# Cosformer attention and a gated layer on one core: q, k, v of batch 0 also cast to fp16 by GpSimd's loads, first products by 128 tokens, normalising in three steps

## The chip, the cores and the metric

The kernel runs on one core of one Trainium2 chip. A core has TensorE (PE, matmuls; its weight loads are listed as PEld), VectorE (DVE), ScalarE (ACT), GpSimd (POOL) and SyncE (SP); SP, ACT and POOL can issue DMAs, and all DMAs share 16 DMA engines. The metric is the device time of one execution in microseconds (us), the median of several runs. Lower is better.

## The reference

q, k, v are fp32 of shape 8 batches x 8 heads x 576 tokens x 64. The result is 4608 x 512 in fp32.

```python
def phi(x, c, s):                                  # c, s: cos and sin of pi/2 * token / 576
    r = np.maximum(x, 0.0)
    return np.concatenate([r * c, r * s], axis=-1) # 64 -> 128 features
q_p, k_p = phi(q, cos_w, sin_w), phi(k, cos_w, sin_w)
kv  = np.einsum('bhsf,bhsd->bhfd', k_p, v)
z   = np.sum(k_p, axis=2)
num = np.einsum('bhsf,bhfd->bhsd', q_p, kv)
den = np.einsum('bhsf,bhf->bhs', q_p, z)[..., None] + 1e-06
x   = (num / den), heads side by side              # 4608 tokens x 512
h   = x @ w_in                                     # 512 -> 2048
out = (h * np.cos(h)) @ w_out                      # 2048 -> 512
```

## The kernel before

**Tiling.** A batch's 576 tokens are 4 tiles of 128 tokens and a rest of 64; the rests of two batches share a fifth tile (t = 4). Layer 1 and layer 2 are done batch by batch in chunks c = 0 to 7 of 512 tokens, and a ninth chunk holds all the rests. Inside SBUF a token block of five or four tokens lies on each partition, so a load of q, k or v is two DMAs: `five` (5 tokens on 64 partitions) and `four` (4 tokens on the other 64). What the missing fifth token leaves is set to zero.

**Attention of a batch.** `load` (L264) brings q, k, v. `prep` (L286) computes relu times cos or sin, one instruction for a token tile and one of the two feature halves, on ACT or DVE, and writes fp16 into KQ. `cast_v` (L300) copies v into V1, which has a column of ones for z. `kv` (L311) multiplies k with V1, 40 matmuls (L319), and copies the result to kvz. q must be transposed: in batches 0 and 1 by PE (`q_pe`, L348, and a copy of the result by ACT or DVE, L352 or L354), from batch 2 on by a transposing DMA that SP issues (`q_dma`, L358). `num` (L365) computes numerators and denominators (L380) into PSUM and normalises: `norm` adds 1e-6 to the denominators (L412), takes reciprocals (L414) and multiplies (L405), one step of the plan, all on DVE. `x_pe` (L430) or `x_dma` transposes x into xT.

**Layers.** In chunks 0 and 1 `layer1` (L473) takes two 128-column blocks of w_in and half of the tokens (256) at a time: 8 matmuls of 256 columns (L493) into a bank of PSUM. `gate` (L464) computes the cosine on ACT (L467) and multiplies on DVE (L469). From chunk 3 on, parts of layer 1 and all of layer 2 are done with 7 products in place of 8 (L620, L796). Stores of the result are issued by POOL (L683).

**Batch 0.** Its q, k, v (in that order, `ORDER0`) are loaded as fp32 by SP into tiles that are used for something else later (`raw0`, L206 to L209). All other loads of q, k, v are issued by POOL and cast to fp16 on the way, as are w_in (`weights`, L873, four DMAs of a quarter) and w_out (`w_out_load`, L884). A small copy on POOL (`hold`, L875), which waits for batch 0's k, stands ahead of w_in's loads. POOL sets S2, V1 and MINUS at the beginning (L855, L860, L861).

**Dummy matmuls.** `warm` (L866) runs matmuls on constants: 14 at the beginning, 16 behind the q transposes of batch 0, and 4, 3 and 2 between the numerators of batch 0 (`FILL`).

**What sets the order.** Each step is recorded in a plan with its cost, due time and what it reads and writes. The list `ORDER` of 1348 words, written into the file, fixes the order of all steps, and for steps that may run on two engines, the engine. Each engine works its instructions in order. POOL's DMAs use 8 semaphores in turn, so a DMA can wait for the landing of the one eight before it.

Of the kernel before, what the change touches and what calls it, by code (L numbers as in the profile page):

```python
# [10 lines left out]
AF = mybir.ActivationFunctionType  # L11
ALU = mybir.AluOpType
# [5 lines left out]
POW = False  # L18
FAST = ((3, 2), (4, 2), (5, 2), (6, 4), (7, 4), (8, 4))
ORDER = (  # L20
    "1 6 1 -3 4 -6 7 1 1 1 1 1 18 1 -5 -7 -1 14 -5 -4 107D 1A -109 6 -25 17 -19 33 1D 8A 92 -136 "
    "38A 4D 93 -92D -3A 5D -31 27A -2D -24 22D 10A 3A -1D -3D 2A -23 -9 37D 2A -1D 2 -4A -1D 86 "
    "-115 35 1 -32 -9 42 -29 30 -26 27 77 -75 -1 -44 49 -1 3 -1 72 -76 9 -8 7 3 -1 67 -71 8 -7 8 "
    "1 59 -63 7 -6 65 9D -18 -49 63D 1D -67 62 -57 -4 3 71D -12 -55 -2 62D -61 4 -2 1 4 -2 57D "
    "-56 4 -2 58D -57 4 -2 54D -53 4 -2 50D -49 4 -2 50D -49 4 -2 175 -122D -4A -48 4 171 -173 "
    "63D -58 -2 -2 3 2 2 43A 4D -48 4 -2 38D -33 -4 2 55D -54 4 -2 53A -2D -50 36 -34 54 -14A 13D "
    "-52 4 47D -1D -21 6D 123 -104 -24 4 6D -3 18 -12D -2 -3 117 -93 -20 15 4 -5 101 -112 13 23 "
    "75 -110 17 -47 51 -1 -7 24 -68 45 8 14 710 -721 13 -8 90D -89 716 -721 -3 -5 100D -79 -20 8 "
    "86A 2A 2D 4D -93 88A -84 26 64A -81 73D -85 267 -272 95D 4D 117 -207 91D -69 -21 207 -182 "
    "82D -15 -70 188 -183 -19 15 75A 113 -120 -65 2 2 681 -617A -65 4 -2 73D -72 4 -2 66D -5A -60 "  # L30
    "4 -2 59 -27 24 -51 -36 91D -86 32 -5 61 -59 30 144A -205 32 60A 118A -175 58 1A -32 -26 61A "
    "-1 -54 -41 202A -4 -196 34 2 60 112A -11 -162 62 1 -61 -32 94 106A 6A -151 43 -1 -2 103A "
    "-200 101 -64 61 -63 172A -102 -104 38 159D -160 4 -2 311 -145A -165 63 -2 -59 2 158D -97 95A "
    "-153 55 244 -303 2 63 1 -3 4 -62 -51 119 101A -100 -4 232 -238 4 238 -299 62 -66 3 159 -157 "
    "161D 3A -67 -96 159A -209 140 78A -7 -99 31 -2 6 65D -95 27 -2 72 2A -68 59 12D -101 90 148D "
    "-136 135D -134A -76 4 -36 104 -62 -5 72A 135D -132 -73 -1 5 67 123 12D -134 -71 4 1 187 5A "
    "-196 10 -48 110 -230 163 2 190A -349 158 67 2 -64 -44 -2 230A -121 -61 63 -68 197A -235 42 "
    "65 -68 69 1 -65 5 61 119A -183 4 -5 66 117A -116 1 -115 53 -4 67 122A -184 69 109A -172 57 "
    "-67 5 314 -250 -118 117 -62 -53 239A 130 -252 -59 2 305 -123A -121 -67 7 309 -311 178 -182 7 "
    "-186 364A -238 54 187A -91 6 -4 2 88 -249 241 -79 91A -73 66 -82 -158 161 -40 38 4 -46 128D "  # L40
    "-83 -160 150 12 -4 5 -11 21 -8 -45 55 200A -133A -68 -172 375A -131D -245 2 244 2A -85 208A "
    "-188 -18 -159 237 -9 -231 163 2 -48 -115 2 240A -78 81 -83 84 113 -239 59 -176 -4 122 126 "
    "-77 203A -256 241 -187 -55 134 -245 363A -119 -65 188A -197 -10 -47 133 112A 149 -332 -61 53 "
    "9 71 -248 119 1 49 71 -59 68 -131 132 111A -240 49 8 66 -60 174D -107 -69 -59 60 196A -13D "
    "-114 2 -75 74 -60 -71 133 -83 -48 70 -9 71 -70 -61 1 61 193A -7D -185 -61 254 -21D -165 168A "
    "-173 -17 -44 60 315 -313 11 175A 126 -311 190A -186 -68 255A -184 87 -89 91 88A -86 -92 173 "
    "-168 171D -174 175 -83 -88 87 -157 67 185A -8 -85 -163 255A -98 7 76 -113 127 -75 63 -114 38 "
    "91 -252 162 216A -382 169 -5 -159 253 -91 90 -251 173 -50 130 -91 -161 123 256A -206 201A "
    "-223 -156 259 -90 -1 20 186 -204 90 -71 -59 131 -90 -172 180 202A -255 246 -110 2 -70 189A "
    "-210 200 -201 23 68 -5 -73 -11 -45 69 67 -134 49 197A -202 91 2 -1 -133 47 5 199D 1A -251 "  # L50
    "134 -79 -58 250A -112 -88 9 196A -250 50 -4 -50 63 76 -75 74 -133 238A 2D -179 -63 64 335 "
    "-351 8 12 69 -134 1 396 -142A -253 60 338 -334 186D -184 -5 -9 347 -334 4 -2 -5 200A -15 13A "
    "-188 91 -93 -2 183A -176 184D -188 181 -85 -91 89 83 -247 167 -95 96 92 -97 99D -90 235A "
    "-238 -163 247A -180 100 1 80 1D -254 75 99 -5 -37 45 -46 116 -241 398A -226 85 138A -226 -5 "
    "-169 254A -79 -169 257 -262 254 -72 -175 256 -130 50 -6 -176 183 -48 26 230 -261 6 256 -128 "
    "-131 -2 -130 177 -44 131 -88 2 5 213A -204 -13 5 -46 127 -72 -54 260A -214 83 -128 127 -69 "
    "197D -126 -75 5 -13 219A -210 75 1 1 -85 -51 66 -2 -4 213D -147 -121 132 -72 214A -226 214D "
    "-137 150A -228 16 190A -191 -59 130 -84 15 213A -207 -20 15 52 146D -196 -11 -52 256A 16 "
    "-210 2 -67 277D -199 -77 67 2 -66 68 196A -12D -177 -4 -4 198 -196 -78 269 7A 7 -268 270A "
    "-206 2 94 -90 190A -98 -6 -161 72 94 101 -105 98 -92 18 75 -130 42 -41 52 -10 -168 179 -22 "  # L60
    "-30 44 10 91 -421 420 -113 7 108 -87 -20 18 -183 168 3 96A -266 273 1 -106 -41 56 92 -114 12 "
    "12 -192 181 -12 114 -105 15 -192 283 1 -103 -47 144 -276 191 10 -68 -134 284 -84 73 -80 8 -4 "
    "-66 75 79 -87 -63 68 83 -109 -38 69 -14 13 -71 63 10 78 -102 -47 83 -84 82 -24 -9 -46 148 "
    "-68 -10 -69 1 69 -7 85 -67 69 -75 -20 16 5 10 -82 68 15 -23 20 -7 -75 83 -3 6 94 -179 180 "
    "-93 -1 -16 76 39 -105 103 -95 3 93 -182 69 21 -88 -1 86 -84 88 88 23 -18 16 -20 7 14 -113 "
    "101 17 -199 196 -15 -42 44 -182 199 -203 181 23 -61 46 16 -61 43 -182 201 -18 -38 -5 45 -334 "
    "337 14 1 -14 -193 146 44 4 17 -3 6 -2 -31 35 -1 -2 -63 67 16 49 -62 -29 -44 74 13 -10 -79 3 "
    "74 -23 40 -16 12 -35 -48 88 -87 83 -235 217 7 1 -17 -203 235 -14 16 -1 39 -127 90 -14 53 "
    "-132 136 -56 14 -90 77 -76 128 -74 75 -128 129 2 -39 -91 133 -45 4 43 -1 -41 -92 69 -9 87 "
    "-12 -65 75 -9 10 -145 77 59 -49 60 3 -13 14 -150 151 -64 53 -134 135 -64 -70 84 -90 7 120 14 "  # L70
    "-140 90 60 -15 -127 143 9 -8 -310 250 69 -34 -126 156 5 -4 -155 150 -8 14 7 -159 86 74 -13 9 "
    "16 -9 -2 -77 90 -12 -74 85 -44 35 1 10 -86 -2 43 39 -78 87 -183 95 90 -32 -56 47 40 -30 -56 "
    "89 -88 72 -71 75 11 -10 -75 61 26 -16 17 -26 -60 70 -71 91 -12 -77 86 4 -88 89 -4 -86 2 75 "
    "-71 -3 4 84 -87 88 5 -89 -3 82 11 -88 90 -1 -5 -85 86 6 -8 15 -12 7 6 -7 3 5 -6 2 8 -7 8 -4 "
    "5 1 1 -6 10 -9 8 -2 1 3 1 1 1 1 1 1 "
)


class Plan:


    def __init__(self):
        self.steps = []
# [940 lines left out]
```

## Time and profile before

| | |
|---|---|
| median of 3 runs | 280.96 us (278.95, 280.96, 282.47) |
| the profiled execution's own time | 283.07 us |
| its span, first to last instruction | 281.3 us |
| PE, PEld busy | 269.9 us (96%), 216.4 us (77%) |
| DVE, ACT, POOL busy | 251.8 us (90%), 210.5 us (75%), 60.3 us (21%) |
| mean granted TensorE clock | 0.994 |
| DMA queue of POOL (q0) | 29856 packets, 28.12 MB |
| DMA queue of SP (q1) | 47840 packets, 14.95 MB |

How to read it: times inside the profile count from the span's start. The span and the time of the same execution differ by 1.77 us, which lie around the span. PE's busy time is modelled from pipelined matmuls and is not PE at its peak. MB of a casting load are those written, half of those read. The granted clock is the share of TensorE's full speed that it was allowed.

### The profile page before, as it was taken

To read this page: it belongs to the slowest core of one execution; us is meant where nothing else is said; L and a number is where in the kernel's file an instruction comes from. 1 tells how busy PE (TensorE), PEld (TensorE's weight loads), DVE (VectorE), ACT (ScalarE), POOL (GpSimd) and SP (SyncE) were. 2 spreads that over 40 slices of the span, in tenths; PEclk is the share of its full clock that TensorE was granted. 3 is DMA by queue.
4 is the path that set the end of the run, shared out by engine and by line. 5 is a ranking of instruction groups with operands and counts; after the bars stand their busy time and mean duration, and the time that the engine had idled before them with its cause. 6 is when DMAs were issued, how large, how long until landed. Compare 5 with 4: busy or idle time off the path is not lost.

```text
span 281.3 us, 6759 instructions
## 1 busy us (share of the span) xinstructions
PE 269.9 (96%) x2691; PEld 216.4 (77%) x2691; DVE 251.8 (90%) x484; ACT 210.5 (75%) x353; POOL 60.3 (21%) x98
## 2 busy tenths in 40 slices
PE   7799999998999799999999999999999999999994
PEld 2568876865956478787878787779988888888883
DVE  2879999897999799999999999999999999988952
ACT  2856876898899969889899987987576776657420
POOL 1472141410403300502323030002110220121300
PEclk9799999999999999999999999999999999999999
DMA  6999999999999999999999999486850434075124
GB/s 208 327 201 203 201 190 177 184 147 185 125 188 156 193 226 145 193 172 156 210 199 107 179 189 161 77 166 150 192 94 2 87 107 125 3 224 114 75 77 149
DMA packets 78463, 44.06 MB, mean 157 GB/s; under 512 B 46176, under 2 KB 75360, under 8 KB 78432
## 3 DMA queue, kind: packets, MB, share of 16 engines
q0 software_dynamic: 29856, 28.12, 57.5%
q1 hardware_dynamic: 47840, 14.95, 30.9%
q10 hardware_dynamic: 736, 0.57, 0.6%
q8 instruction: 21, 0.34, 0.5%
q14 instruction: 10, 0.08, 0.1%
HBM read 36.74 MB, written 9.44 MB: 164 GB/s over the span
## 4 chain that ended last, share of the span: by engine, by line
PE 82%; DMA 9%; DVE 5%; ACT 2%; issue 1%; SPq 0%; ACTq 0%
PE M L796 33%; PE M L620 14%; PE M L525 8%; DMA qT<-KQ 7%; PE TR L620 6%; PE M L493 4%; PE M L722 4%; PE ATT L380 3%; DVE gT L469 3%; PE ATT L319 3%; DMA gT<-in_q_dram 2%; PE TR L525 2%; PE M L348 2%; PE ATT L870 1%; ACT KQ L295 1%
## 5 line engine op out<-in xcount | busy, mean ns | idle before, releaser
L796 PEld LDWEIGHTS <-gT 128*128 128x128 f16 x560 | 54.1, 98 | 7.6
L295 ACT ACTIVATE KQ<-RAW,CS 128x512 f16<-128x512 f16 x86 | 59.1, 720 | 0.0
L796 PE MATMUL M<-w_out_sb,gT 128*128 128x256 f16 x448 | 56.2, 273 | 0.0
L467 ACT ACTIVATE ch<-M 128x512 f32<-128x512 f32 x75 | 44.1, 598 | 13.2 <-PE M L493 4.4
L469 DVE TENSOR_TENSOR gT<-M,ch 128x512 f16<-128x512 f32 x73 | 49.1, 684 | 3.1 <-ACT ch L467 2.3
L525 PE MATMUL M<-xT,w_in_sb 128*128 128x512 f16 x136 | 33.1, 379 | 0.0
L796 PE MATMUL M<-TT,S 128*128 128x256 f16 x256 | 32.0, 273 | 0.0
L807 ACT ACTIVATE ost<-M 128x512 f32<-128x512 f32 x32 | 19.1, 597 | 17.2 <-PE M L796 13.4
L493 PE MATMUL M<-xT,w_in_sb 128*128 128x256 f16 x256 | 29.7, 272 | 0.0
L683 POOL DMA_DIRECT2D out_dram<-ost x32 | 18.8, 611 | 47.2 <-DVE ost L811 25.7
L620 PEld LDWEIGHTS <-w_in_sb 128*128 128x128 f16 x264 | 25.4, 98 | 3.7
L796 PEld LDWEIGHTS <-S 128*128 128x128 f16 x256 | 24.6, 98 | 3.0
L628 ACT ACTIVATE Z<-M 128x512 f32<-128x512 f32 x31 | 18.2, 600 | 11.6 <-PE M L620 8.6
L493 PEld LDWEIGHTS <-w_in_sb 128*128 128x128 f16 x256 | 24.6, 98 | 3.0
L632 DVE TENSOR_TENSOR Z<-M,Z 128x512 f32<-128x512 f32 x38 | 25.4, 683 | 1.1 <-PE M L620 0.6
L525 PEld LDWEIGHTS <-w_in_sb 128*128 128x128 f16 x160 | 14.8, 98 | 13.1
L405 DVE TENSOR_TENSOR x<-ATT,rec 128x512 f16<-128x512 f32 x32 | 22.1, 691 | 1.1
L380 PEld LDWEIGHTS <-qT 128*128 128x128 f16 x320 | 15.7, 98 | 7.3 <-DMA qT<-KQ 3.7
L811 DVE TENSOR_TENSOR ost<-M,ost 128x512 f32<-128x512 f32 x24 | 16.4, 684 | 4.2 <-PE M L796 4.0
L380 PE MATMUL ATT<-kvz,qT 128*128 128x65 f16 x288 | 16.4, 194 | 3.0 <-DMA qT<-KQ 2.6
L296 DVE TENSOR_SCALAR KQ<-RAW,CS 128x512 f16<-128x512 f16 x54 | 18.3, 350 | 0.2 <-DMA RAW<-in_k_dram 0.2
L773 DVE TENSOR_TENSOR S<-gT 128x2048 f16<-128x2048 f16 x14 | 17.0, 1217 | 0.1
(133 smaller groups left out, 482.3 us busy)
## 6 DMA issues: line engine op xcount, KB each, us to landing
out_dram<-ost POOLq DMA_DIRECT2D x32, 256.0 KB, 4.7
RAW<-in_k_dram POOLq DMA_DIRECT2D x7, 320.0 KB, 5.3
RAW<-in_q_dram POOLq DMA_DIRECT2D x7, 320.0 KB, 7.6
w_in_sb<-in_moe_w_in_dram POOLq DMA_DIRECT2D x4, 512.0 KB, 9.8
w_out_sb<-in_moe_w_out_dram POOLq DMA_DIRECT2D x4, 512.0 KB, 12.1
RAW<-in_v_dram POOLq DMA_DIRECT2D x6, 320.0 KB, 7.4
RAW<-in_k_dram POOLq DMA_DIRECT2D x7, 256.0 KB, 6.4
RAW<-in_q_dram POOLq DMA_DIRECT2D x7, 256.0 KB, 6.7
```

What stands on the lines that cost most here:

```text
L295: fn = {"ACT": lambda: nc.scalar.activation(out=out_, in_=in_, func=AF.Relu, scale=sc), "DVE": lambda: nc.vector.tensor_scalar(out=out_, i ...
L380: nc.tensor.matmul(bank[hb][:, hh * D1:(hh + 1) * D1], lhsT=a[:, h, :], rhs=z[:, h, :], start=(i == 0), stop=(i == len(parts) - 1))
L405: nc.vector.tensor_tensor(out=split(x16[n][:, hs, :], k), in0=A[:, :, :, 0:D], in1=split(rec[n][:, hs], k).unsqueeze(3).broadcast_to((P, k ...
L467: act(0.5, due, lambda: nc.scalar.activation(out=ch[c], in_=bank, func=AF.Sin, bias=math.pi / 2.0, scale=1.0), [key], [("ch", c)])
L469: mul(due, 0.61, lambda q: q.tensor_tensor(out=dst, in0=bank.rearrange("p (j s) -> p j s", j=2), in1=ch[c].rearrange("p (j s) -> p j s", j ...
L493: nc.tensor.matmul(M1[m][:, jj * 2 * P:(jj + 1) * 2 * P], lhsT=w_in_sb[:, cc, j * P:(j + 1) * P], rhs=X[:, cc, ts], start=(cc == 0), stop= ...
L525: nc.tensor.matmul(M, lhsT=w_in_sb[:, cc, j * P:(j + 1) * P], rhs=X[:, cc, :], start=(cc == 0), stop=(cc == NCT - 1))
L620: nc.tensor.matmul(bank[0][:, j * TH:(j + 1) * TH], lhsT=a(cc, j), rhs=b[:, cc, :], start=(first and j == 0 and cc == 0), stop=(last and j ...
L632: dve(0.61, due + 0.3, lambda: nc.vector.tensor_tensor(out=dst, in0=bank[0], in1=dst, op=ALU.add), [bank[1], key], [key])
L683: pl.add(eng, 0.9 if eng == "POOL" else 0.65, 0, due, lambda: q.dma_start(out=dst, in_=src_), keys, [], dma=(nb, 355.0))
L796: nc.tensor.matmul(bank[0][:, tt * MH:(tt + 1) * MH], lhsT=a[:, j, tt * P:(tt + 1) * P], rhs=b[:, j, :], start=(first and (apart or tt == ...
L807: act(0.5, due, lambda: nc.scalar.activation(out=dst, in_=view(bank), func=AF.Copy), [bank[1]], dk)
```

## The change

All loads of q, k, v are now issued by POOL and cast to fp16; `raw0` and the fp32 forms of `prep` and `cast_v` are gone. In batches 0 and 1, v is loaded by halves of the heads (as batch 1's was before) and q in two pieces of tokens (0 and 1; 2 to 4), so that q's runs of contiguous data become 2 or 3 tokens long. Batch 0's k comes first, then v and q. `hold` is gone, w_in's first quarter comes in two halves, the other three whole. The settings of S2, V1 and MINUS move from POOL to DVE. The opening run of dummy matmuls is 19 instead of 14, and the later ones are gone. In `layer1` of chunks 0 and 1, the products with w_in's first quarter are done for 128 tokens at a time, so that each needs one tile of xT only; the other quarters stay as they were. Normalising becomes three steps of the plan: the sums on DVE or ACT, the reciprocals on DVE or as a power of -1 on POOL, the multiplication on DVE. kvz of batches 0 and 1 is copied in two halves, each by ACT or DVE, and the numerators of a half of the heads need only the kvz of that half. Costs and due times of the plan change, and `ORDER` is another list of 1417 words.

What this makes of the built program: DVE has 15 sums (40 before), 24 reciprocals (36), 73 preparations (66, of them 12 from fp32); ACT has 25 sums (none before) and 87 preparations (94); POOL has 12 powers, a library reload ahead of the first of them, and its first DMA waits for DVE's third memset (the one of k's missing token).

```diff
-    home0 = {"k": gT[0].rearrange("p h t j s -> p (h t j s)"),
...
-    def load(b, nm, due, hs=(slice(0, H),)):
...
-        q, eng = (nc.sync, "SP") if b == 0 else (nc.gpsimd, "POOL")
...
+    def load(b, nm, due, hs=slice(0, H), ts=range(NT + 1)):
+
+        m, n = raw[nm], b % 2
+        five, four = tokens(src[nm][b])
+        heads = range(H)[hs]
+        for ap, k, x in ((four, NT, 1 - n), (five, NT + 1, n)):
+            t = slice(ts[0], min(ts[-1] + 1, k))
+            dst, ap = blocks(m, x)[:, hs, t, :], ap[:, hs, t, :]
+            wr = [((nm, h, i), x) for h in heads for i in sorted({min(j, 2) // 2 for j in ts})]
+            pl.add("POOL", 0.72, 0, due, lambda dst=dst, ap=ap: nc.gpsimd.dma_start(out=dst, in_=ap),
...
-        if pair:
-            act(0.4, due, lambda: nc.scalar.activation(
...
+        if b < 2:
+            for i in range(2):
+                o, z = Z[:, i], bank[i][:, 0:HB * D1]
+                either(due, {"ACT": 0.35, "DVE": 0.35}, {
...
-        if POW and pair is None:
-            act(0.2, due, dens, keys, [("den", n)])
-            pl.add("POOL", 0.6, 0.8, due, recs, [("den", n)], [("rec", n)])
-            dve(0.61, due, scaled, keys + [("rec", n)], [("x16", n)])
-        else:
-            dve(1.05 if pair is None else 1.15, due, norm, keys, [("x16", n), ("den", n), ("rec", n)])
+        m = len(cut)
+        either(due, {"DVE": 0.1 + 0.06 * m, "ACT": 0.21 * m}, {"DVE": sums, "ACT": dens}, keys, [("den", n)], False)
+        either(due, {"DVE": 0.2, "POOL": 1.75}, {"DVE": lambda: nc.vector.reciprocal(out=rec[n], in_=den[n]), "POOL": recs},
+               [("den", n)], [("rec", n)], False)
+        dve(0.62 + 0.07 * m, due, scaled, keys + [("rec", n)], [("x16", n)])
...
-                                        M1[m][:, jj * 2 * P:(jj + 1) * 2 * P],
-                                        lhsT=w_in_sb[:, cc, j * P:(j + 1) * P], rhs=X[:, cc, ts],
+                                        M1[m][:, jj * 2 * P + lo:jj * 2 * P + hi],
+                                        lhsT=w_in_sb[:, cc, j * P:(j + 1) * P], rhs=X[:, cc, h0 + lo:h0 + hi],
...
+                        if quarter == 0:
+                            for i in range(2):
+                                pe(2 * NCT, MMT, due, lambda i=i, mm=mm: mm(i * P, (i + 1) * P),
+                                   [xk[2 * hf + i]] + wk + [("M1", m)] * i, [("M1", m, 1)] if i else [("M1", m)])
+                        else:
+                            pe(2 * NCT, MMH, due, lambda mm=mm: mm(0, 2 * P), xk[2 * hf:2 * hf + 2] + wk,
+                               [("M1", m), ("M1", m, 1)])
...
-        nc.gpsimd.memset(S2[:, 0:2, :], 0.5)
+        nc.vector.memset(S2[:, 0:2, :], 0.5)
         nc.vector.memset(PIH, math.pi / 2.0)
+        for nm in "kvq":
+            nc.vector.memset(raw[nm][:, :, NT, :], 0.0)
+        nc.vector.memset(V1[:, :, :, D], 1.0)
+        nc.vector.memset(MINUS, -1.0)
...
-        pl.add("POOL", 0.4, 0.5, 0, hold, hk(ORDER0[1], b=0), [("w_in", g) for g in range(4)])
         for g in range(4):
...
+            for e in ((0,), (1,)) if g == 0 else ((0, 1),):
...
-        warm(14, 6.5)
...
+        warm(19, 6.1)
+        load(0, "k", 0)
+        for h in HALVES:
+            load(0, "v", 1, h)
+        load(0, "q", 2, ts=(0, 1))
+        weights()
+        load(0, "q", 3, ts=(2, 3, 4))
...
-        warm(16, 3.45, rd=[("TR", 0)])
...
-            if FILL[t]:
-                warm(FILL[t], 0.2157 * FILL[t], M1[1],
...
+        load(1, "k", T)
+        for h in HALVES:
+            load(1, "v", T, h)
+        for ts in ((0, 1), (2, 3, 4)):
+            load(1, "q", T, ts=ts)
```

## The prediction

> **What bounds the kernel now.** Four views, in this order. The engine totals and slices of the page first; then busy time by stretch of time for the start and for everything behind it; then the chain of waits of the first 24 us; then the transfers, read second by second.
>
> ```profile
> PE 269.9 (96%) x2691; PEld 216.4 (77%) x2691; DVE 251.8 (90%) x484; ACT 210.5 (75%) x353; POOL 60.3 (21%) x98
> ...
> DMA  6999999999999999999999999486850434075124
> ```
> PE is the bound. DVE is next.
>
> ```profile
> 5.09:8.50 3.41, 1.47 (x10) 0.62 (x9) 0.98 (x3) 1.00 (x2) 0.00 (x0) 0.99 1.07 370
> 8.50:11.91 3.41, 3.08 (x26) 2.39 (x23) 3.12 (x10) 2.67 (x5) 1.06 (x2) 0.51 1.08 359
> 11.91:15.32 3.41, 3.41 (x22) 1.71 (x21) 3.41 (x11) 2.98 (x8) 3.11 (x5) 1.00 1.20 227
> ...
> 21.50:275.70 254.20, 251.02 (x2526) 204.97 (x2524) 236.61 (x441) 198.33 (x332) 51.05 (x79) 1.00 0.89 149
> ```
> Columns: stretch, length, busy us of PE, PEld, DVE, ACT, POOL, granted clock, DMA share, GB/s. From the first product of layer 1 (21.5) to the last matmul (275.7) PE idles 254.20 - 251.02 = 3.2 us. So the change can win only ahead of 21.5 and in those 3.2 us; the 5.6 us behind 275.7 stay (the last twenty groups of PE, DVE and ACT do the same work in nearly the same order). The clock column matters too: after a stretch in which PE was busy 1.47 of 3.41 us the granted clock is 0.51 for the next 3.41 us, then 1.00 again.
>
> ```profile
> 1.55 5.84 DMA gT<-in_q_dram
> ...
> 7.50 1.96 ACT KQ L295 x3
> ...
> 9.50 1.89 PE M L348 x16
> 11.39 3.76 PE ATT L870 x16
> 15.14 0.45 PE M L348 x8
> 15.59 1.22 PE M L319 x40
> ...
> 21.72 0.87 PE M L493 x8
> ```
> The start is a chain from the q load through preparation, transposes, L319 (k times v), numerators and normalising to L493. Sixteen transposes take 1.89 us at 9.50 (0.118 each), eight take 0.45 at 15.14 (0.056 each): that is the clock. Layer 1 of batch 0 has its first group at 21.56, its fourth done at 25.7 and runs dense from 23.1.
>
> ```profile
> q1 hardware_dynamic: 1614, 1.84, 107.6%
> ...
> q0 software_dynamic: 374, 0.19, 144.4%
> ...
> q0 software_dynamic: 204, 0.21, 125.4%
> ...
> 65.32 0.43 PE L380 MATMUL ATT<-kvz,qT 128*128 128x65 f16 x8 [0.79 <-DMA qT<-KQ]
> ...
> 97.73 0.63 PE L380 MATMUL ATT<-kvz,qT 128*128 128x65 f16 x15 [1.82 <-DMA qT<-KQ]
> ```
> Queue: packets, MB written, share. The first row is 5 to 10 us, when SP's fp32 loads run alone: 1.84 MB in 5 us, 0.365 MB/us. The next two are single microseconds of POOL's casting loads (31 to 32 us, 17 to 18 us): 0.19 and 0.21 MB of fp16, so about 0.203 MB/us, which is 0.406 MB/us of the fp32 source. The transfers never pause until 55 us. The last two rows are PE's two largest idle times after the start, both for a transposing DMA.
>
> **The change part by part.**
>
> *Loads of batch 0.* SP issued eight at 0.73 us and later. Now POOL issues ten, and the first waits for DVE's third memset. DVE starts at 0.81; the memset of S moves to it (0.27 by the fp16 row of RAW to 0.49 by the fp32 row, same element count), then PIH 0.06 and RAW 0.27: 1.4 to 1.65. I take 1.6. From issue to an even flow: SP's loads 2.3 us; POOL's k loads at 128.14 and 152.26, back-reckoned from the bytes moved, 2.7 and 2.2. So flow from 4.0 (3.6 to 4.3) against 3.0. Batch 0 is 1.77 MB of fp16: 8.7 us at 0.203, against 3.54 / 0.365 = 9.7. Start and rate cancel; what counts is the order. In the rows of before a load lands 1.0 us after its bytes by this reckoning (w_in's first quarter: 18.65 and 19.7). A piece of POOL's new order then lands at 4.0 + (MB written up to and with it) / 0.203 + 1.0: k, with a quarter of v between its two DMAs, 0.72 MB, 8.6; the first q pieces 1.15 MB, 10.7; the last of q 1.475 MB, 12.3; the last of v 1.77 MB, 13.7; w_in's first two half-quarters 2.03 and 2.56 MB, 15.0 and 17.6 (a k load of batch 1 between them); the later quarters 3.08, 4.36 and 5.01 MB, 20.2, 26.5 and 29.7. POOL's issues, 0.70 each, keep ahead of this (thirteen more DMAs in all, 9.1 us on an engine busy 21%).
>
> *Small pieces.* q of batches 0 and 1 comes in runs of two or three tokens, 256 and 384 B written. The trace has 512 B (374 packets in one us) and up in casting loads; the transposes' packets move at about 850 per us near 128.5. Price: 0 if bytes rule, and if packets rule 2048 / 374 - 2.9 = 2.6 us a batch. 512 and 1024 B packets move equal MB/us, so I take 0 and keep 2.6. The Trainium skill, DMA: Bandwidth & Descriptors, Specifications, gives 512 B as the smallest transfer at line rate; no run here shows that, and by it the sum below would be some 2.6 us longer.
>
> *The chain to layer 1.* Preparation from fp16 on DVE costs 0.29 back to back (three in 0.87) instead of 0.41 (six in 2.47). PE's opening run is 19 dummy matmuls, 1.3 to about 7.5; the runs of 16, 4, 3 and 2 are gone. PE then idles to 12.5, longer than the idle after which the clock fell, so the transposes of t1, t0 and t2 run at 0.118: 12.5 to 15.35. L319: 15.35 to 15.95, second half behind v's casts (15.8) to 16.55. kvz by ACT 17.05; numerators 17.35; sums on ACT 0.2; two reciprocals 0.4; x0 18.7, x1 19.45; x transposed, copied by ACT behind qT3 (1.02) and one late q preparation (0.71): 20.4 and 21.0. Layer 1 starts at 20.45 with 128 tokens alone; the fourth group ends at 24.65, where it was 25.7. **Term: -1.05.** If the clock does not fall at all it is 23.55: -2.2. If it is low once more as layer 1 starts, half of the next 1.7 us is lost: -0.2. w_in is in time for each.
>
> *First products by 128 tokens.* 64 matmuls at 0.0565 (transposes, same shape) for 32 at 0.109: 3.62 for 3.49. Batch 0 is in the term above; batch 1: **+0.13**.
>
> *Normalising in three steps.* DVE loses 25 sums (23 at 0.158) and 12 reciprocals (0.20), 6.3 us, gains 7 preparations (0.34), and 4.8 in all; ACT gains 25 at about 0.2 and loses 7 preparations at 0.72. PE was never idle for DVE between 100 and 250, so this is worth nothing by itself. POOL gains 12 powers: 0.22 (its 128x8 memset) to 0.53 (its 512-wide one); I take 0.3. New wait: DVE's x waits for POOL, and POOL's queue is in order behind loads and stores. Behind DVE's x stand gates, behind them PE's banks.
>
> *A reload.* The built program has a library reload on POOL just ahead of the first power, behind the last w_out load (about 41.7). No row shows one. Cover: POOL idled 7.4 us there before (43.57 to 50.95), and the first power's sum comes at about 44.9. Below 4 us it is hidden; at 7.4 it holds DVE's x0 some 4 us and PE about 2. I take 0.
>
> *The middle.* After layer 1 of batch 0 (done at 35.7 with half of batch 1's L319, by the lead above), PE now meets the numerators of batch 2 after 19.1 us of work instead of 27.8 (six product groups of layer 1 and two of layer 2 stand behind instead of ahead). With one half of L319 already done that is 54.2, and 54.8 with the short waits below. q of batch 2 lands at 46.6 by the bytes plus 2.5, the slip of the same stretch in before (w_out: 51.8 reckoned, 54.3 landed): 49.1; prepared 50.5; the transposing DMA took 4.3 (median) to 8.1 (the same one in before): 54.8 to 58.6. Wait 0 to 3.8, I take 1.9. The last w_out lands about 54.5, just in time. The wait of 1.82 for batch 3 has more room (needed about 91, first transposes about 51, 3 us apiece). The two short ones at 37 to 39 us (0.54) stay. 0.54 + 1.9 for 3.15: **-0.7**.
>
> Sum: 283.07 (span 281.3 and 1.77 around it) - 1.05 + 0.13 - 0.7 = 281.45. The profiled execution lies 2.11 above the median, so 279.3 against 280.96.
>
> **The rivals.**
>
> *A, the start gains nothing* (0.22). Small pieces cost 2.6 on each of two batches, and the clock is low again in layer 1. The start comes 2.6 + 0.9 later, the last w_out 5.2 later and PE waits some 2 more: 281.9 to 284.8. For it: PE's busy share in the stretch ahead of layer 1 is about 64%, between 43% (clock fell) and 89% (it held); against it: equal MB/us at 512 and 1024 B. The Trainium skill, TensorE: Matmul & The Clock Gate, Part 4, says that transposes do not count as busy for the clock. By that, L319 too would run at 0.061 and the time would be near 280.6; but the trace disagrees: 24 transposes and 0.7 us of matmuls between 8.28 and 11.91 brought 1.00 back.
>
> *B, slower: DVE waits for POOL* (0.13). Five powers (the 3rd, 4th, 8th, 10th, 11th) stand directly behind a load or store that itself waits for DVE, ACT or an earlier transfer; POOL's waits in before ran to 9 us. DVE is busy 28.97 of 30 us at 130 to 160, so a wait beyond about 1 us reaches PE. It passes 2% when they cost PE 7.3 us together, 1.5 each: 286.8. Against it: the order puts the powers well ahead of their x.
>
> *C, all of it works* (0.20). The clock holds and the middle loses its transposing waits: 283.07 - 2.2 + 0.13 - 2.6 - 2.11 = 276.3; flow from 3.6 brings 275.9.
>
> **How the numbers follow.** The forecast has 0.45: 279.3, its own range 277 to 281.5. Low end 275.2, a little under C; high end 285.3, A with 0.5 for the reload. About 2% (5.6 us) is what a measurement of this kernel can tell from no change: faster than 275.3 needs C and 1 us more, 0.13; slower than 286.6 is most of B, 0.10; within, 0.77.
>
> **What would show it.** The matmuls of layer 1 starting near 20.5, granted clock about 0.5 somewhere between 10 and 15 us, the fourth group done by 25; casting loads at 0.2 MB/us with the small pieces among them; PE idle between layer 1's start and the last matmul of 2 to 4 us; no DVE wait for POOL over 1 us. Wrong if layer 1 starts after 22, if PE idles over 6 us in the middle, or if DVE's x shows POOL as its releaser with microseconds beside it.

## The result, and the profile after

The changed kernel is slower: 292.67 us (median of 4; 291.88 to 296.35) against 280.52 for the kernel before (median of 4 beside it; 278.95 to 282.47). The ratio is 1.042, with a 95% interval of 1.033 to 1.051; 279.3 had been predicted. The profiled execution of the changed kernel is the slowest of its four (296.35 us) and in a slower state, which the ratios leave out, so what is said of the cause rests on differences that the profiles of other runs with its order show too (the table at the end of the experiments).

First the page of the changed kernel: engine totals, the granted clock and the transfers in 40 slices.

```profile
PE 270.6 (92%) x2735; PEld 217.1 (74%) x2735; DVE 244.9 (83%) x455; ACT 205.8 (70%) x365; POOL 91.4 (31%) x119
...
PEclk9869999999799999999999999999999999999998
DMA  6999999999999999799995995846981163047034
```

PE has the same work as before (270.6 against 269.9 us) in a longer span, so what grew is PE's idle time. DVE and ACT have less to do, POOL half as much again. The transfers are at nine tenths or more for almost all of the first 118 us (16 slices of 7.4 us).

Next, busy time by stretch. The stretches run from the first matmul of layer 1 to the first of layer 2, and from there to the last matmul. First the kernel before, then the changed one; the columns are those of the prediction.

```profile
21.56:41.08 19.52, 18.98 (x239) 17.26 (x237) 18.27 (x44) 15.74 (x26) 5.19 (x8) 1.00 1.31 200
41.08:277.40 236.32, 233.68 (x2303) 188.95 (x2300) 219.31 (x399) 183.19 (x308) 45.86 (x72) 1.00 0.86 145
```

```profile
22.88:42.84 19.96, 19.41 (x264) 17.50 (x264) 18.33 (x45) 17.37 (x31) 7.58 (x11) 1.00 1.37 200
42.84:290.70 247.86, 236.99 (x2346) 190.05 (x2342) 215.70 (x375) 179.76 (x320) 68.95 (x83) 0.99 0.83 139
```

Of 13.3 us in the profiles, 1.3 lie ahead of layer 1, 0.4 between layers 1 and 2 of batch 0, and 11.5 behind that. There PE idles 247.86 - 236.99 = 10.9 us, where it idled 236.32 - 233.68 = 2.6. (In the runs e2, e3 and e8 below, which keep this order, it is 7.1 to 9.1 us.)

The timeline of PE in the changed kernel shows where (bracketed: idle time before the matmul, and what ended it).

```profile
57.95 0.30 PE L371 MATMUL ATT<-kvz,qT 128*128 128x65 f16 x4
...
63.99 0.43 PE L371 MATMUL ATT<-kvz,qT 128*128 128x65 f16 x8 [0.39 <-DVE ost L731]
68.88 0.43 PE L371 MATMUL ATT<-kvz,qT 128*128 128x65 f16 x8 [0.77 <-DMA qT<-KQ]
74.43 0.55 PE L371 MATMUL ATT<-kvz,qT 128*128 128x65 f16 x8 [3.15 <-DMA qT<-KQ]
...
99.40 0.43 PE L371 MATMUL ATT<-kvz,qT 128*128 128x65 f16 x8 [2.21 <-DMA qT<-KQ]
```

These are numerators. Batch 2's first stand 7.4 us earlier than before (57.95, where it was 65.32), but those of its fourth tile come at 74.43, where the kernel before had them at 73.49 without a wait:

```profile
73.49 0.42 PE L380 MATMUL ATT<-kvz,qT 128*128 128x65 f16 x8
```

Batches 3, 5 and 6 have such waits too, of 0.36 to 2.2 us. After the 3.15 us the granted clock fell: the eight matmuls of 512 columns at 74.78 took 3.46 us instead of 1.89.

The chain of waits of the changed kernel names the transfer that PE waited for at 74.43, and the start that was predicted to be shorter.

```profile
2.00 1.47 POOL RAW L269 x2
3.47 6.91 DMA RAW<-in_k_dram
...
14.21 2.74 PE M L339 x24
16.95 2.20 PE M L309 x40
...
22.88 1.11 PE M L480 x16
...
63.64 10.75 DMA qT<-KQ
74.38 0.05 issue
74.43 0.55 PE ATT L371 x8
```

One transposing DMA took 10.75 us. At the start, k landed 6.9 us after its second DMA was issued, and the transposes of q and k times v ran at the low clock (24 transposes 2.74 us).

Last, the powers, in the page's costliest groups.

```profile
L392 POOL TENSOR_TENSOR rec<-den,MINUS 128x8 f32<-128x8 f32 x12 | 23.4, 1953 | 44.4 <-ACT den L388 25.8
...
L396 DVE TENSOR_TENSOR x<-ATT,rec 128x512 f16<-128x512 f32 x32 | 21.9, 686 | 2.6 <-POOL rec L392 1.6
```

A power takes 1.95 us on average, not 0.3. DVE nonetheless waited for POOL only 1.6 us in all.

### The profile page after: what moved, and what is told of

Its sections match the earlier page's. It is cut to its first block, busy times and chain, and to the rows that moved or that the text cites. A ratio compares the mean times of both kernels' runs of the same rounds, so it can differ in the third digit from the quotient of the medians.

```text
span 294.6 us, 6886 instructions
## 1 busy us (share of the span) xinstructions
PE 270.6 (92%) x2735; PEld 217.1 (74%) x2735; DVE 244.9 (83%) x455; ACT 205.8 (70%) x365; POOL 91.4 (31%) x119
## 4 chain that ended last, share of the span: by engine, by line
PE 67%; DMA 17%; ACT 5%; DVE 4%; POOL 2%; issue 2%; SPq 1%; ACTq 0%; DVEq 0%
PE M L792 27%; PE M L616 11%; DMA qT<-KQ 11%; PE M L518 6%; PE TR L616 5%; PE M L480 4%; PE M L719 4%; PE ATT L371 3%; DMA RAW<-in_v_dram 2%; DMA RAW<-in_k_dram 2%; PE ATT L309 2%; ACT ch L455 2%; DMA out_dram<-ost 2%; PE TR L518 1%; PE M L339 1%
## 5 line engine op out<-in xcount | busy, mean ns | idle before, releaser
L285 ACT ACTIVATE KQ<-RAW,CS 128x512 f16<-128x512 f16 x87 | 60.8, 724 | 13.3 <-issue 7.3
L392 POOL TENSOR_TENSOR rec<-den,MINUS 128x8 f32<-128x8 f32 x12 | 23.4, 1953 | 44.4 <-ACT den L388 25.8
L480 PE MATMUL M<-xT,w_in_sb 128*128 128x256 f16 (+1 forms) x320 | 30.9, 251 | 0.4 <-ACT xT L429 0.2
L286 DVE TENSOR_SCALAR KQ<-RAW,CS 128x512 f16<-128x512 f16 x73 | 23.8, 354 | 8.9 <-DMA RAW<-in_k_dram 8.5
L480 PEld LDWEIGHTS <-w_in_sb 128*128 128x128 f16 x320 | 25.9, 98 | 4.0 <-issue 1.2
L616 PEld LDWEIGHTS <-w_in_sb 128*128 128x128 f16 x264 | 25.3, 98 | 3.9
L371 PE MATMUL ATT<-kvz,qT 128*128 128x65 f16 x288 | 16.5, 196 | 10.7 <-DMA qT<-KQ 8.3
L269 POOL DMA_DIRECT2D RAW<-in_q_dram x20 | 13.9, 705 | 35.2 <-ACT KQ L285 20.6
L518 PEld LDWEIGHTS <-w_in_sb 128*128 128x128 f16 x160 | 15.2, 98 | 12.6
L269 POOL DMA_DIRECT2D RAW<-in_k_dram x16 | 11.5, 721 | 29.6 <-ACT KQ L285 11.9
```

Of the source, the lines that this page charges most:

```text
L269: pl.add("POOL", 0.72, 0, due, lambda dst=dst, ap=ap: nc.gpsimd.dma_start(out=dst, in_=ap), (), wr, dma=(len(heads) * R * D * 4 / 1e3 * (t ...
L285: fn = {"ACT": lambda: nc.scalar.activation(out=out_, in_=in_, func=AF.Relu, scale=sc), "DVE": lambda: nc.vector.tensor_scalar(out=out_, i ...
L286: "DVE": lambda: nc.vector.tensor_scalar(out=out_, in0=in_, scalar1=0.0, scalar2=sc, op0=ALU.max, op1=ALU.mult)}
L371: nc.tensor.matmul(bank[hb][:, hh * D1:(hh + 1) * D1], lhsT=a[:, h, :], rhs=z[:, h, :], start=(i == 0), stop=(i == len(parts) - 1))
L392: nc.gpsimd.tensor_tensor(out=rec[n], in0=den[n], in1=MINUS, op=ALU.pow)
L480: nc.tensor.matmul(M1[m][:, jj * 2 * P + lo:jj * 2 * P + hi], lhsT=w_in_sb[:, cc, j * P:(j + 1) * P], rhs=X[:, cc, h0 + lo:h0 + hi], start ...
```

## The experiments

Three theories stood at the beginning. P: the powers hold POOL's queue, and with it the loads of later batches. O (called T in the first expectation): the new order asks for numerators of batch 2 and later too soon after their transposing DMAs were issued. S: the start (clock, late loads, tiles shared by batches 0 and 1) carries the loss on. Later X was added: transposing DMAs are slow because casting loads run beside them.

### Without powers (e1)

```diff
             e = eng or next(iter(s["opts"]))
+            if e == "POOL" and "DVE" in s["opts"]:
+                e = "DVE"
```

> The changed kernel with its twelve powers on POOL done as reciprocals on DVE (0.20 us each, 2.4 us more on DVE). Theory P (the powers): a power takes about 2 us, waits for its sum at the head of POOL's queue, and the loads of the next batch stand behind it (v of batch 3 goes out at 62.6 where its tile was free by 56). Without powers v of batch 3 goes out before 58, PE's idle time between layer 1 and its last matmul falls from 11.4 us to 6 or less, and the time from 292.7 to 286 to 288. Theory T (the transposing DMAs come too late for the new order, whatever POOL does): the idle time stays above 9 us and the time at 291 to 293.

Measured: 295.08 us (ratio 1.050, 1.042 to 1.058). v of batch 3 did go out earlier, at 54.1. PE's idle time behind the first product of layer 2 is 13.4 us (249.06 - 235.62), 11.0 of it for transposing DMAs. Theory P falls: without powers the kernel is no faster.

### Start: clock (e2) and tiles (e3)

```diff
-        warm(19, 6.1)
+        warm(37, 6.1)
```

> The changed kernel with 37 dummy matmuls at the opening in place of 19, so that PE is busy to about 12 us instead of 8.1. Theory C (the clock): PE's 6.1 us of idle time brings the granted clock of 0.5 at 15 to 18.4 us, in which 24 transposes took 2.7 us and 40 matmuls of k with v 2.2 us; with the clock held these take 1.4 and 1.4, layer 1 starts near 21.2 instead of 22.9 and the time falls by 1 to 2 us, to about 291. Rival L (the loads): the last v piece and DVE's casts hold k times v in any case, layer 1 starts at 22.3 or later and the time falls by less than 0.6 us.

Measured: 290.67 us (ratio 1.033, 1.028 to 1.039; the interval overlaps the changed kernel's). The clock held throughout, the 24 transposes took 1.79 us, layer 1 started at 20.32. But layer 2 started at 42.85, as in the changed kernel, after waits of 0.99 us for a gate and 1.07 for w_out. The 2 us came behind that: 241.65 us to the last matmul with 7.1 idle. What the clock gave was used up before layer 2. Batch 2 has no wait here (e3 has one of 2.61 us), with the same order and all its loads: its last transposing DMA, issued at 62.59, landed at 69.63, just ahead of its numerators.

```profile
69.68 0.43 PE L371 MATMUL ATT<-kvz,qT 128*128 128x65 f16 x8
```

Later batches wait instead (1.58 us at 82.05, 2.76 at 106.77). So where the waits fall differs from run to run, and only their sum behind layer 2 can be compared.

```diff
-        m, n = raw[nm], b % 2
+        m, n = (raw if b else raw0)[nm], b % 2
```

> The changed kernel with tiles of their own for batch 0's q, k, v (in fp16, in the memory where the kernel before had them), so that batch 1's first load needn't wait until DVE has prepared batch 0's k. In the changed kernel that wait is 2.9 us at the head of POOL's queue (14.36), w_in's second half and all loads of batch 1 stand behind it, and the transfers drop to 0.06 MB/us for 15 to 16 us. If that gap matters, the loads behind it go out some 1.5 us earlier and the time falls by about 1 us; if layer 1's start is set by batch 0's chain alone and later loads have room, the start stays at 22.9 and the time changes by less than 0.5 us.

Measured: 292.13 us (ratio 1.039, 1.032 to 1.047), 0.5 us below the changed kernel, no more than the noise: the gap is gone (0.20 MB from 15 to 16 us, where it was 0.06), and nothing shows that it mattered here. So S explains at most e2's 2 us of the 12.

### Batch 0 by SP again (e4)

```diff
+    raw0 = {nm: heads_tokens(t.bitcast(F32)[:, 0:NR]) for nm, t in home0.items()}
...
+            pl.add("POOL", 0.72, 0, due, lambda dst=dst, ap=ap: (nc.gpsimd if b else nc.sync).dma_start(out=dst, in_=ap),
```

> The changed kernel with batch 0's loads undone: SP issues them in fp32 into tiles of their own, in the changed kernel's order and pieces, DVE and ACT prepare from fp32, and POOL holds w_in back until the first half of v is there. If POOL's late and slow beginning (first load at 2.0, 32 GB/s in the first 5 us) set the start, k lands near 8.5 instead of 10.4, the transposes begin near 12.5 instead of 14.2, layer 1 starts near 21.5 and the time falls by 1 to 2 us. If half the bytes make up for it, the start stays within 0.5 us of 22.9. The idle time in the middle stays above 8 us in either case.

Measured: 295.69 us (ratio 1.053, 1.047 to 1.058), 3 us more than the changed kernel. The transposes began at 14.75, layer 1 at 24.16 after a wait of 1.52 for w_in. Both expectations of the start were wrong; the idle time behind layer 2, 8.2 us, is above 8 as expected. In this order the casting loads are the better ones: with SP's loads, behind which POOL holds w_in, PE waits for the weights.

### The old order behind the start (h1), with 256 tokens, with powers

The list `ORDER` was rebuilt: each step that both kernels have takes the old place, and the steps of batch 0 up to its fourth product group the new one. Only the list, which also names the engines (all reciprocals and nearly all sums on DVE, a few preparations on another engine), and the 37 dummy matmuls differ from the changed kernel.

> All edits of the changed kernel but the powers, with 37 dummy matmuls at the opening and another order: batch 0's steps up to its first four product groups stand as in the changed kernel, everything behind them stands in the order of the kernel before (sums and reciprocals on DVE, in the place where normalising stood). Theory O (the new order behind the start is what costs): the numerators of batch 2 and later again have as much work ahead of them as before, PE idles 3 to 5 us between layer 1 and the last matmul instead of 11.4, layer 1 starts near 20.4, and the time is 279 to 281.5. Rival E (the edits themselves, such as half-size pieces and loads that share tiles, delay the transfers of the later batches): PE still idles 8 us or more and the time stays above 286.

Measured: 291.99 us (ratio 1.040, 1.035 to 1.045). The time did not fall, but it lies elsewhere:

```profile
20.56:50.50 29.94, 22.91 (x272) 20.17 (x272) 20.06 (x51) 16.09 (x27) 8.26 (x13) 0.89 1.09 157
50.50:286.30 235.80, 234.17 (x2335) 189.22 (x2332) 218.58 (x398) 182.91 (x307) 45.53 (x71) 1.00 0.92 145
```

From layer 1 to layer 2 it took 29.9 us instead of 19.5. The chain shows batch 1's k landing at 25.3 while its preparations stand in DVE's queue ahead of x and the gates. Behind layer 2 the run is as quick as the kernel before (235.8 us, 1.6 idle). That speaks for O behind layer 2, but layer 2 begins at 50.50 here instead of 42.84, so that the transfers had more time. It also says that the new loads need the new order of batch 1.

```diff
-                                pe(2 * NCT, MMT, due, lambda i=i, mm=mm: mm(i * P, (i + 1) * P),
+                                pe(2 * NCT, MMT, due, lambda i=i, mm=mm: mm(0, 2 * P) if i else None,
```

> The run before with the first products of batches 0 and 1 by 256 tokens again (the instruction count of PE falls by 64). By 128 tokens layer 1 can start when the first tile of x is there, 0.9 us ahead of the second in the changed kernel's trace, and costs 0.26 us more for the two batches: with 256 tokens the start is 0.5 to 1 us later and the time 0.3 to 0.8 us longer. If the groups behind wait for the fourth tile in any case, the time is 0.1 to 0.3 us shorter.

Measured: 291.86 us (ratio 1.039, 1.034 to 1.044), the same; layer 1 started 0.39 us later and nothing came of it.

> The first of these runs with the changed kernel's twelve powers on POOL and its sums on ACT again, the multiplication on DVE put just ahead of x's transposition. If powers of 2 us on POOL cost time by themselves (DVE waits for them, or loads stand behind them), the time is 2 us or more above the first run; if POOL's idle time takes them, within 1 us of it.

Measured: 314.46 us (ratio 1.120, 1.113 to 1.127), 22 us more. With x directly behind its power, DVE waited 10.7 us for POOL and PE 17.5 for x: the new wait of rival B exists, and in the changed kernel, whose order puts the powers further ahead of x, DVE waited 1.6 us.

### Less traffic beside the transposing DMAs (e6)

```diff
-            pl.add("POOL", 0.72, 0, due, lambda dst=dst, ap=ap: nc.gpsimd.dma_start(out=dst, in_=ap),
+            pl.add("POOL", 0.72, 0, due, lambda dst=dst, ap=ap: b == 3 and nm in "vq" or nc.gpsimd.dma_start(out=dst, in_=ap),
```

> The changed kernel without the loads of v and q of batch 3 (0.59 MB, issued at 62.6 to 65.4; the values of batch 2 are used again, so batch 3's result is not the reference's). Theory X: the transposing DMAs of batch 2 are slow (6 to 10.8 us each) because casting loads run beside them. Without these loads they take 5 us or less, PE's waits of 0.8 and 3.2 us at 68.9 and 74.4 shrink to under 1 us together, the granted clock stays at 1.00 there, and the time falls by 4 to 6 us with the clock. Rival: transposing DMAs queue behind one another, five in a row at about 5 us each; then the waits stay above 3 us and the time within 1.5 us of 292.7.

Measured: 286.24 us (ratio 1.020, 1.015 to 1.025), 6.4 us less, with those loads left out. Batch 2's numerators ran at 56.66 to 68.32 with no wait for a DMA, and the clock stayed at 1.00. That alone would not decide, since e2 had no wait there either. The transfers of two stretches of 2 us, first in the changed kernel (70 to 72 us), then in this run (62 to 64), show more; q0 is POOL's queue, q1 holds SP's transposing DMAs, and columns are packets, MB, share:

```profile
q0 software_dynamic: 433, 0.26, 89.0%
q1 hardware_dynamic: 429, 0.11, 43.3%
```

```profile
q1 hardware_dynamic: 2146, 0.53, 123.8%
```

Alone the transposing DMAs move 2146 packets in 2 us, beside casting loads 429. The Trainium skill, DMA: Bandwidth & Descriptors, section Queues, rings and completion order, says that each DMA engine takes turns between its queues packet by packet. Its packet is a bundle of several descriptors, which need not be what the profile counts; 433 against 429 fits taking turns, and no run here shows the bundles. POOL's packets are the larger ones (0.26 MB for 0.11), so a transposing DMA that meets them gets a third of the time (43.3 of 132.3). Theory X holds; the rival, five in a row at 5 us each, falls, since in this run four that were issued from 56.27 to 61.74 landed from 62.06 to 64.91, about 1 us apart.

The kernel before shares its DMA engines in the same way; from 90 to 92 us:

```profile
q0 software_dynamic: 457, 0.25, 87.1%
q1 hardware_dynamic: 449, 0.11, 43.3%
```

One of its transposing DMAs took 11.7 us, longer than any of the changed kernel's, and cost PE 1.82 us. So the sharing is not new; what is left to show is that the order has too little work to cover it.

### The old order from layer 2 on (h2), with own tiles

As h1, but all of batch 0's and batch 1's attention keep the new order. Layer 2 begins at 43.26, as in the changed kernel (42.84) and in e2 (42.85).

> As the first of the runs before (all edits but the powers, 37 dummy matmuls), but the new order is kept for all of batch 0 and for batch 1's attention, and the order of the kernel before begins with layer 2 of batch 0. That run lost its time between 20 and 50 us, where preparations of batch 1 stood in DVE's queue ahead of the gates while k of batch 1 landed only at 25.3; behind 52 us PE idled 1.5 us in place of 10.8. Theory O (numerators of batch 2 and later, ordered closer to their transposing DMAs, are what costs): PE idles under 3 us behind 45 us, layer 1 starts near 20.4, the first product of layer 2 at 42 to 43 as in the run with 37 dummy matmuls, and the time is 281 to 284, some 8 us below that run's 290.7. If the edits' transfers are what costs, PE's waits for transposing DMAs come back and the time stays above 288.

Measured: 285.88 us (ratio 1.017, 1.013 to 1.022), 4.8 below the run with 37 dummy matmuls; 8 had been expected, and 281 to 284 us. From that run the order differs, with the engines that it names; the reciprocals on DVE gained nothing in e1, though no run has the new order with both edits at once. PE idles 2.7 us behind the first product of layer 2, where the runs with the new order have 7.1 to 13.4. Theory O is shown: it is the order of the steps from batch 2 on that put the waits there.

> The run before with tiles of its own for batch 0's q, k, v, so that batch 1's loads and w_in needn't wait for batch 0's preparation. The loads behind go out 1 to 2 us earlier, PE's waits between 20 and 43 us (2.5 us in the run with 37 dummy matmuls) fall by 1 us or more, and the time is 280 to 282.5. If nothing waits for those loads, it is the same within 0.5 us.

Measured: 284.29 us (ratio 1.013, 1.008 to 1.018), above the expected 280 to 282.5. The same stretches as above:

```profile
21.36:41.18 19.82, 19.31 (x264) 17.50 (x264) 17.68 (x44) 17.35 (x31) 7.49 (x11) 1.00 1.37 200
41.18:279.20 238.02, 235.22 (x2346) 190.03 (x2342) 218.55 (x396) 184.41 (x312) 45.51 (x71) 1.00 0.89 145
```

PE idles 2.8 us in the long stretch, and its numerators of batch 2 stand at 67.58 to 75.74 without a wait:

```profile
67.58 0.42 PE L374 MATMUL ATT<-kvz,qT 128*128 128x65 f16 x8
...
75.74 0.42 PE L374 MATMUL ATT<-kvz,qT 128*128 128x65 f16 x8
```

Its transposing DMAs for batches 2 and 3 are no quicker than e2's (3.3 to 8.5 us, against 3.2 to 7.0), so it is not their speed that the old order mends. From the issue of batch 2's first one to the first numerators there are 7.3 us here and 8.2 in the kernel before (0.79 of it waiting), but 5.0 in the changed kernel and in e2. This is the best version with the change's loads, and still above the kernel before.

### Moving the wait in the changed kernel (e7, e8)

```diff
+            for h in range(H):
+                nc.tensor.matmul(ps[:, h, :], lhsT=qp[:, t, h].rearrange("p g d -> p (g d)"),
+                                 rhs=IDENT, is_transpose=True)
+            nc.scalar.activation(out=dst, in_=ps, func=AF.Copy)
+        pl.add("SP", 1.25, 0, due, by_pe if b == 2 else lambda: nc.sync.dma_start(
```

> The changed kernel with q of batch 2 transposed by PE (five times eight transposes into PSUM, 2.3 us of PE, and five copies on ACT of 1.0 us) in place of five transposing DMAs; the loads of batch 3 stay. Theory X (transposing DMAs stand behind casting loads): PE's waits of 0.8 and 3.2 us at 68.9 and 74.4 and the low clock behind them (1.7 us) go, the five DMAs leave room for the loads of batch 3, and the time is 287 to 290 against 292.7. If it was batch 3's loads themselves or the preparation of q that held PE, as could be read into the run without them, the waits stay under another name and the time is 292 to 296.

Measured: 297.08 us (ratio 1.057, 1.048 to 1.067), 4.4 more. Batch 2's waits for DMAs went, but none of that was kept: PE has 2.5 us more to do behind layer 2, and batch 3 waits 2.42, batch 4 1.16 and 0.50, batch 6 1.31. On POOL, v of batch 3 stood behind a power whose sum came at 62.1, and went out at 63.7: the DMA engines had been nearly empty (8 GB/s in the slice from 58.9 to 66.2). The number of theory X was wrong here.

```diff
+            hold = (lambda: nc.gpsimd.tensor_copy(out=HOLD[0:1, :], in_=qT[3][0:1, 0, 0:1])) if (
+                b == 3 and nm == "v" and k == NT + 1) else (lambda: None)
```

> The changed kernel with the loads of v and q of batch 3 held back on POOL until the fourth transposing DMA of batch 2 has landed; nothing is left out. If only the sequence of transfers is wrong, these DMAs take about 3 us each, PE's waits at 68.9 and 74.4 go (5.6 us with the clock), the loads go out some 4 us later, of which batch 3 gives back 0 to 3 us at 99 to 103, and the time is 287 to 290. If the DMA engines are full through this stretch in any sequence, the waits only move to batch 3 and the time stays at 291 to 294.

Measured: 291.73 us (ratio 1.042, 1.035 to 1.049), within a microsecond of the changed kernel. Batch 2's waits went (the copy on POOL was released at 64.29), and batch 3 waits 1.94 and 1.51 us in their place, batch 5 another 1.51. The second expectation held: with this order the transfers are short of time from batch to batch, in this sequence too.

### What is left of the loss (h3, b1, h4, h5)

h3 has 47 dummy matmuls in h2's place with own tiles; b1 is the kernel before with the first products by 128 tokens; h4 is h3 by 256 tokens; h5 is h4 with batch 0 by SP in fp32.

> The run with the old order from layer 2 on and own tiles (284.3), with 47 dummy matmuls at the opening in place of 37. There PE still idled 2.5 us ahead of the transposes and the granted clock fell to 0.5 in the products of k with v (2.4 us in place of 1.4) and the numerators. If the clock is what is left of the start's loss, layer 1 starts near 20.2 instead of 21.4, and the time falls by 1 to 1.5 us, to 283. If the start has room, it stays within 0.5 us of 284.3.

Measured: 284.76 us (ratio 1.017, 1.013 to 1.021). The clock held, layer 1 started at 20.70, layer 2 at 40.93, and the time stayed: the start has room.

> The kernel before with nothing changed but the first products of batches 0 and 1, by 128 tokens in place of 256 (64 more matmuls). If this part costs what its rows say, the two batches take 0.26 us more, of which batch 0 may gain up to 0.5 us back by starting at its second tile of x: 280.3 to 281.3. If it is what is left of the loss (3.5 us) of the run with the old order, 283 or more.

Measured: 281.85 us (ratio 1.008, 1.004 to 1.012): 1.6 us more in the medians, where the rows give 0.26.

> The run with own tiles, 47 dummy matmuls and the old order from layer 2 on (284.8, 1.7% above the kernel before), with the first products by 256 tokens again. If the products by 128 tokens cost 1.6 to 2.2 us, as they did in the kernel before, the time falls to 282.5 to 283.2; if they cost nothing, as the pair with the old order behind the start said, it stays within 0.6 us of 284.8.

Measured: 287.34 us (ratio 1.022, 1.015 to 1.028): by 256 tokens the median is 2.6 us higher here, with layer 1 at 21.46, but the two ratios' intervals overlap. With h1's pair (no difference) and b1 the three results on this part point three ways; its size is not settled.

> The run before, and batch 0's q, k, v loaded in fp32 by SP again, with POOL's w_in held until the first half of v is there; of the change's edits then only the split normalising without powers, q in pieces and batch 0's order are left. If the casting loads of batch 0 make up the rest, layer 1 starts near 21 and the time is 280 to 282. If they help, as they did in the changed kernel's own order (3.6 us), it rises above 285.

Measured: 292.83 us, the median of six from 288.46 to 297.01 (ratio 1.034, 1.027 to 1.041, from the three up to 291.84). The casting loads help in this order, too; layer 1 waited 2.36 us for w_in, as it waited 1.52 in e4.

A table of the runs that carry the conclusion. "Long stretch" is from the first product of layer 2 to the last matmul, and "idle" is PE's idle time in it. Times are medians, and the kernel before, run beside each group of runs, lay at 280.15 to 280.98; e1's, h1's and h2's runs have all reciprocals on DVE.

| kernel | order behind layer 2 | time, us | layer 1 at | layer 2 at | long stretch | idle |
|---|---|---|---|---|---|---|
| before | old | 280.52 | 21.56 | 41.08 | 236.3 | 2.6 |
| changed | new | 292.67 | 22.88 | 42.84 | 247.9 | 10.9 |
| e1, no powers | new | 295.08 | 20.62 | 40.94 | 249.1 | 13.4 |
| e2, 37 dummies | new | 290.67 | 20.32 | 42.85 | 241.7 | 7.1 |
| e3, own tiles | new | 292.13 | 22.17 | 42.10 | 242.7 | 7.9 |
| e8, loads held | new | 291.73 | 21.21 | 41.14 | 244.5 | 9.1 |
| h1 | old | 291.99 | 20.56 | 50.50 | 235.8 | 1.6 |
| h2 | old | 285.88 | 19.85 | 43.26 | 237.4 | 2.7 |
| h2, own tiles | old | 284.29 | 21.36 | 41.18 | 238.0 | 2.8 |

## Why the prediction was wrong, point by point

**What bounds the kernel.** Right as far as it went: PE is the bound and only its idle time can change. But the view of the transfers was read too weakly. "The transfers never pause until 55 us" stood there, and the page of the kernel before has the DMA slices full for much longer; that the DMA engines are a second bound, which decides when a transposing DMA lands, was not drawn from it. A small slip beside it: 275.7 is about where the last group of matmuls begins; it ends at 277.4, with the same idle time ahead of it.

**Start, -1.05.** In the profiled execution +1.32. The opening was the same in e1, e6, e7 and e8, where layer 1 started at 20.6 to 21.4, so the term varies from -0.9 to +1.3 from run to run, and layer 2 started at 40.9 to 41.5 in those four, against 41.08: nothing was won. Two steps of the term were mis-sized. k was to land at 8.6; it landed at 10.38 (its second DMA took 6.91 us), and at 8.8 to 9.4 in e1, e6, e7 and e8. The ten DMAs did land in the order of issue, but the flow was slower to begin than reckoned: 0.02 MB from 3 to 4 us, 0.10 in the next, 0.19 from 5 on. What held k up further in the profiled execution is open. And the low clock was to last for the transposes of 12.5 to 15.35; in the profiled execution it lasted until 20, so that k times v took 2.41 instead of 1.37 (2.27 and 2.41 in e6 and e8, 1.55 in e1).

**Small pieces, 0.** Right. While the q pieces came, the queue moved more packets at the same rate: from 10 to 11 us

```profile
q0 software_dynamic: 597, 0.19, 168.8%
```

against 0.19 MB in 375 packets from 6 to 7 us. The Trainium skill has 512 B as the least for line rate (DMA: Bandwidth & Descriptors, Specifications), by which the sum would have been 2.6 us longer; no loss shows at these 256 and 384 B written. They are 512 and 768 B of fp32 read, so if the bytes read count, the run doesn't test it.

**First products by 128, +0.13 for a batch.** Not settled (above).

**Normalising, 0.** The price was wrong by a factor of six: 1.95 us (1.66 to 3.65) lies outside both bounds, 0.22 and 0.53, which came from memsets. A power is not a memset, and the upper bound should have said so; the plan's own cost for it, 1.75, stood in the diff. The conclusion held: DVE waited 1.6 us for POOL, not the 7.3 that rival B needed, and e1 shows nothing to be won without powers.

**The reload, 0.** Right: POOL stood idle 2.36 us ahead of the first power, which began 0.08 us after its sum was there. What the reload itself takes within that time is not shown.

**The middle, -0.7: the step that failed.** It read: "the transposing DMA took 4.3 (median) to 8.1 ... Wait 0 to 3.8, I take 1.9", and of batch 3 that its wait "has more room". PE's idle time behind layer 2 rose by 8.2 us instead, and by 4.4 to 6.5 in e2, e3 and e8. The step priced one transposing DMA, the first, for which its range held: it landed at 57.90, and the numerators ran at 57.95. Those of the other three tiles landed at 63.94, 68.83 and 74.38, each just ahead of its numerators, because they shared the DMA engines with one another and with casting loads, those of batch 3 at the end; e6 shows the sharing, h2 that the order makes it matter. The step also took the numerators of batch 2 as one date, where the new order spreads four tiles over 11.7 us without waits (e2) and 16.5 with them. And it did not repeat the reckoning for the later batches, whose waits (2.21 and 0.48 in batch 3, 1.33 in batch 5, 0.36 in batch 6) were again for transposing DMAs. In the profiled execution a further 1.6 us is the clock that fell after the 3.15 us of idle time; e1, e2 and e3 did not have that. One number that the step took from the kernel before is also off: w_out's last two pieces landed there at 53.61 and 55.58, not at 54.3, which changes little.

**The rivals.** None of them was it. A had a late start and 2 us of waiting in the middle; the waiting was four times that. B had the right sign with another mechanism (and its 279.3 + 7.3 makes 286.6, not 286.8). No rival had PE waiting for transposing DMAs in batch after batch, though the prediction's own list of what would prove it wrong ("PE idles over 6 us in the middle") had the idle time.

**Open.** With the old order from layer 2 on and own tiles, 3.5 us remain in the medians (1.3%, 0.8 to 1.8) and 1.8 in the spans (283.1 against 281.3). Neither the clock (h3) nor the products (b1, h4) nor the loads (h5) explain them. Waiting is not what is left: in the long stretch PE idles 2.8 us (2.6 before) but is busy 235.2 (233.7 before), with 43 more matmuls. At least 40 of them are batch 1's first products by 128 tokens (32 more) and the transposes of a tile of q (8) that now stand behind layer 2; b1, with the same products, is busy 233.6 there, so those don't account for it.

## What to carry to other kernels

Where the DMA engines are full, as they were here, an order that asks for transferred data sooner gains nothing and takes away the work that covered the wait: for every such transfer, and not the first alone, compare what else is in the queues between its issue and its use. A price for an operation that the trace does not show wants a bound from a row of the same operation class, and a distance to its consumer that survives the upper bound. A start that gets faster by 2 us, as in e2, is worth nothing if the next stage waits for something else; follow the gain to a point that both traces share.

## What the runs showed of the hardware

- A power of 128x8 values on POOL took 1.66 to 3.65 us in the changed kernel, a reciprocal of the same on DVE 0.20.
- Transposing DMAs moved 2146 packets (0.53 MB) in 2 us alone (e6), 267 GB/s, and 429 beside casting loads; from issue to landing one of the changed kernel took 3.1 to 10.7 us. The Trainium skill (DMA: Bandwidth & Descriptors, Latency and other measured facts) has 261 GB/s for a DMA transpose with a non-contiguous middle dimension. The run's 267 is close to it; whether this transpose counts as such a case is not shown.
- The length of PE's idle time alone did not decide whether the granted clock fell. After 3.15 us (changed kernel, 74.4), 2.42 (e7, 85.2) and 2.00 (e4, 109.9) in the middle of dense work it was 0.50 to 0.51 for about 3.4 us; after 2.93 us (e1, 65.0), 2.76 (e2, 106.8) and 2.61 (e3, 71.6) it stayed at 1.00.
